# Linear attention on one core: loads with 64 reads of 8 KB and 128 writes of 4 KB

## The chip, the cores and the metric

The kernel runs on one core of a Trainium2 chip. The metric is device time in microseconds (us) of one execution; lower is better. A core has five engines with queues of their own (PE: matrix products and weight loads; DVE: vector work; ACT: activation functions; POOL; SP, which here only issues transfers) and 16 DMA engines that move data between memory (HBM) and the on-chip SBUF of 128 partitions.

## The reference

For each of 32 heads, with q, k, v of 2048 x 128 in bf16:

```python
phi_q = where(q > 0, q + 1, exp(q)) + 1e-6
phi_k = where(k > 0, k + 1, exp(k)) + 1e-6
kv  = einsum("sd,se->de", phi_k, v)          # 128 x 128 per head
z   = phi_k summed over s                    # 128 per head
out = (phi_q @ kv) / (phi_q @ z + 1e-6)
```

## The kernel before

One head is one unit of work. Its k, v and q are loaded with one transfer each of 512 KB: partition p holds rows 16p to 16p+15 of the head, 4 KB in one run (`rows`). k_sb, v_sb and q_sb have six buffers each (`NBI`), o_sb has ten (`NBO`).

For one head: ACT computes exp(k) into ek_sb (L368); DVE makes emk_sb = min(exp(k), 1) + 1e-6 (L382); POOL makes rk_sb = relu(k) (L372) and adds emk_sb to it for some of the 16 row tiles (L390), so that phi_k = emk + rk enters PE either as a sum or as two products. PE accumulates kv and z in kvz_ps (L413, L320; a column of ones beside v gives z); ACT copies them to kvs_sb (L430). PE transposes q into xT_ps (L436); ACT and DVE make emq_sb and rq_sb from it (L447, L454, L456, L468). PE multiplies both with kvs_sb into o_ps (L483, L484), DVE takes the reciprocal of the denominator and divides (L506 to L524; for the last two heads ACT divides part of it, L536), and SP stores o_sb (L571).

The order on each engine comes from keys: `Plan.add` takes an operation with a key, each engine runs its operations in the order of their keys, and waits between engines are derived from the buffers that operations read and write. All loads and stores are issued by SP from one queue, in the order of their keys. A load of head h has a key about six heads ahead and waits until its buffer is free. A store's key grows faster than the heads, so that stores are put off more and more behind loads:

```python
late = h + 1.0 + 0.18 * h
```

The store of head 29 is in three parts of 51, 13 and 64 partitions (`PARTS`), that of head 31 in two halves by columns. After its last issue SP waits for all stores to land (L226).

The loads are made by `load` (L361 is its `dma_start`), called for k, v and q of every head; v's buffer has a gap of 32 columns (`GAP`) of which one column of ones is used.

Of the kernel before, what the change touches and what calls it, by code (L numbers as in the profile page):

```python
# [7 lines left out]
P = 128  # L8
# [4 lines left out]
def _ap(base: bass.AP, elem_offset: int, dims):  # L13
    return bass.AP(base.tensor, base.offset + elem_offset, [list(base.ap[0])] + [list(d) for d in dims])
# [217 lines left out]
def bass_standalone__linear_attn_elu__prompt_kernel(  # L232
# [6 lines left out]
    B, H, S, D = q.shape  # L239
    assert D == P and S == 16 * P  # L240
    NT = 16
# [13 lines left out]
    EVEN, ODD = tuple(range(0, NT, 2)), tuple(range(1, NT, 2))  # L255
    MORE = (4, 6, 8, 10, 12, 14)
    GAP = 32
    VW = NT * D + GAP

    qf = q.rearrange("b h s d -> (b h) s d")  # L260
# [4 lines left out]
    with ExitStack() as es:  # L265
        def sb(name, shape, dt):
            return es.enter_context(nc.sbuf_tensor(name, shape, dt))

        k_sb = sb("k_sb", [P, NBI, NT * D], bf16)
        v_sb = sb("v_sb", [P, NBI, VW], bf16)  # L270
        q_sb = sb("q_sb", [P, NBI, NT * D], bf16)
# [29 lines left out]
        pl = Plan()  # L301

        def rows(x, h):
            return x[h].rearrange("(p j) d -> p (j d)", j=NT)
# [11 lines left out]
               reads=[("id0",)], writes=[("ident",)])  # L316
        pl.add("pool", -7, lambda g: g.memset(_ap(vfull, 0, [[VW, NBI], [1, GAP]]), 1.0), writes=[("vones",)])

# [32 lines left out]
        for h in range(NH):  # L351
# [3 lines left out]
            bi, b2, b3, bo = h % NBI, h % 2, h % 3, h % NBO  # L355

            def load(name, buf, src, key, h=h, bi=bi):
                dst, rws = buf[:, bi], rows(src, h)
                if name == "v":
                    dst = v_sb[:, bi, GAP:]  # L360
                pl.add("sp", key, lambda sp: sp.dma_start(dst, rws), writes=[(name, bi)] + ([("vo", bi)] if name == "v" else []), dma=(name, bi))  # L361

            load("k", k_sb, kf, h - NBI - (1.0 if h < 3 else 1.85 if h == 3 else 1.95))
            load("v", v_sb, vf, h - NBI - 0.8)
            load("q", q_sb, qf, h - NBI - 0.9)

            pl.add("act", at("ek", -2.8),
                   lambda a, bi=bi, b2=b2: a.activation(ek_sb[:, b2, :], k_sb[:, bi, :], ACT.Exp),  # L368
# [36 lines left out]
            def kv(pe, tiles, start=False, stop=False, h=h, bi=bi, b3=b3, both_of=both_of):  # L405
                for j in tiles:
                    both = j in both_of or (j in ODD and j not in ADD and h > 0)
                    for src in (emk_sb, rk_sb) if both else (rk_sb,):
                        first, fin = start and j == tiles[0] and src is (emk_sb if both else rk_sb), stop and j == tiles[-1] and src is rk_sb
                        w = src[:, b3, j * D:(j + 1) * D]  # L410
                        l = j == 0 or (j in ODD and h > 0)
                        c = GAP + j * D
                        last = pe.matmul(kvz_ps[:, 1 - l:NC], lhsT=w, rhs=v_sb[:, bi, c - l:c + D], start=first, stop=fin,  # L413
# [11 lines left out]
            if h:  # L425
                pl.add("pool", h + 0.6, lambda g, bi=bi: g.memset(_ap(vfull, bi * VW + GAP + D - 1, [[2 * D, NT // 2], [1, 1]]), 1.0),
                       reads=[("v", bi)], writes=[("vo", bi)], kind="vo")
# [187 lines left out]
```

## Time and profile before

| | |
|---|---|
| time, median of 3 runs | 168.16 us (167.96 to 168.21) |
| the profiled execution | 167.82 us, of which the span of the profile is 166.5 us |
| moved over the DMA queue of SP | 67.12 MB in 18592 packets: 50.33 MB read from HBM, 16.78 MB written to it |
| mean rate over the span | 404 GB/s |
| busy | PE 94%, DVE 91%, ACT 93%, POOL 64% of the span |
| a load or a store, issue to landing, median | 15 us |

The span runs from the first instruction to the last event of the program. "Busy" leaves out waiting and issuing. A DMA packet in the records is one piece of one transfer on one DMA engine: 128 pieces of 4 KB for a transfer of 512 KB, eight on each of the 16 engines, and one small packet per engine that raises the semaphore. A transfer has landed when all 16 engines have raised it.

### The profile page before, as it was taken

The page shows a single profiled execution, that of the slowest core. Times are in us where ns is not written, and L with a number is a line of the kernel's source. Part 1 is how long each engine was busy: PE and PEld are TensorE (multiplying, and loading weights), DVE is VectorE, ACT ScalarE, POOL GpSimd, SP SyncE. Part 2 cuts the span into 40 slices and gives each one's busy share as a digit, 9 for nine tenths or more (in the row PEclk, how much of TensorE's full clock was granted, in tenths as well). Part 3 has the DMA queues.
Part 4 walks back from the last instruction along what each step waited for, and adds up shares of the span by engine and source line. Part 5 has one row for each costly group of instructions (what it writes and reads, how often), then busy time and mean ns, then how long its engine had stood idle before and what let it go on. Part 6 is the DMA issues. An engine that isn't in the chain of part 4 may idle for free.

```text
span 166.5 us, 6269 instructions
## 1 busy us (share of the span) xinstructions
PE 156.0 (94%) x2819; PEld 145.3 (87%) x2453; DVE 152.3 (91%) x270; ACT 155.0 (93%) x143; POOL 106.3 (64%) x128
## 2 busy tenths in 40 slices
PE   7789999999999999999999999999999999999960
PEld 0259999999999999899999989999998999999950
DVE  0587999999999999999999999999999999999991
ACT  3979999999999999999999999999999999998790
POOL 2405788676767877676778867676787767677300
PEclk9999999999999999999999999999999999999998
DMA  5999999999999999999999999999999999999986
GB/s 205 345 417 421 413 415 419 412 407 418 417 416 419 422 417 417 422 421 411 424 420 414 423 421 415 419 421 415 422 420 416 422 421 418 418 421 418 415 310 239
DMA packets 18605, 67.25 MB, mean 404 GB/s; under 512 B 2082, under 2 KB 2210, under 8 KB 18594
## 3 DMA queue, kind: packets, MB, share of 16 engines
q1 hardware_dynamic: 18592, 67.12, 99.4%
q8 instruction: 5, 0.08, 0.2%
q14 instruction: 6, 0.05, 0.1%
q10 hardware_dynamic: 2, 0.00, 0.0%
HBM read 50.33 MB, written 16.78 MB: 403 GB/s over the span
## 4 chain that ended last, share of the span: by engine, by line
DVE 58%; PE 17%; POOL 12%; ACT 6%; issue 3%; DMA 2%; DVEq 0%
DVE o_sb L524 20%; POOL rk_sb L390 12%; DVE rq_sb L456 11%; DVE emk_sb L382 10%; DVE emq_sb L468 9%; PE kvz_ps L413 6%; PE o_ps L483 5%; PE o_ps L484 5%; ACT ek_sb L368 3%; DVE rden_sb L512 3%; DVE o_sb L517 3%; ACT eq_sb L447 2%; DMA k_sb<-in_k_dram 2%; DVE den_sb L506 2%; DVE rk_sb L390 1%
## 5 line engine op out<-in xcount | busy, mean ns | idle before, releaser
L413 PE MATMUL kvz_ps<-v_sb,rk_sb 128*128 128x129 bf16 (+1 forms) x512 | 67.0, 220 | 2.8 <-DVE rk_sb L390 1.0
L524 DVE TENSOR_TENSOR o_sb<-o_ps,rden_sb 128x768 bf16<-128x768 f32 (+2 forms) x62 | 67.8, 1135 | 0.0
L390 POOL TENSOR_TENSOR rk_sb<-rk_sb,emk_sb 128x640 bf16<-128x640 bf16 x30 | 41.9, 1395 | 39.5 <-DVE emq_sb L468 38.2
L372 POOL TENSOR_SCALAR rk_sb<-k_sb 128x1024 bf16<-128x1024 bf16 (+1 forms) x60 | 64.1, 1068 | 2.5 <-DMA k_sb<-in_k_dram 2.5
L483 PE MATMUL o_ps<-kvs_sb,emq_sb 128*128 128x129 bf16 (+1 forms) x536 | 65.2, 217 | 0.0
L484 PE MATMUL o_ps<-kvs_sb,rq_sb 128*128 128x129 bf16 (+1 forms) x536 | 64.4, 217 | 0.0
L368 ACT ACTIVATE ek_sb<-k_sb 128x2048 bf16<-128x2048 bf16 x32 | 61.0, 1907 | 2.6 <-DMA k_sb<-in_k_dram 2.6
L447 ACT ACTIVATE eq_sb<-xT_ps 128x2048 bf16<-128x2048 bf16 (+1 forms) x33 | 60.0, 1821 | 2.0 <-PE xT_ps L436 2.0
L413 PE MATMUL kvz_ps<-v_sb,emk_sb 128*128 128x129 bf16 (+1 forms) x338 | 53.3, 221 | 0.6 <-DVE emk_sb L382 0.3
L413 PEld LDWEIGHTS kvz_ps<-v_sb,rk_sb 128*128 128x128 bf16 x512 | 46.1, 98 | 7.6 <-POOL rk_sb L390 2.7
L483 PEld LDWEIGHTS o_ps<-kvs_sb,emq_sb 128*128 128x128 bf16 x536 | 51.2, 98 | 0.8 <-issue 0.3
L484 PEld LDWEIGHTS o_ps<-kvs_sb,rq_sb 128*128 128x128 bf16 x536 | 51.3, 98 | 0.0
L436 PE MATMUL xT_ps<-ident,q_sb 128*128 128x128 bf16 x512 | 33.8, 219 | 0.6 <-DMA q_sb<-in_q_dram 0.4
L436 PEld LDWEIGHTS xT_ps<-ident,q_sb 128*128 128x128 bf16 x512 | 29.9, 98 | 5.1 <-DMA q_sb<-in_q_dram 4.2
L413 PEld LDWEIGHTS kvz_ps<-v_sb,emk_sb 128*128 128x128 bf16 x338 | 32.5, 98 | 0.9 <-DVE emk_sb L382 0.5
L320 PE MATMUL kvz_ps<-ones_sb,rk_sb 128*128 128x1 bf16 x232 | 31.3, 165 | 0.0
L454 ACT ACTIVATE rq_sb<-xT_ps 128x1024 bf16<-128x1024 bf16 x30 | 30.9, 1029 | 0.0
L382 DVE TENSOR_SCALAR emk_sb<-ek_sb 128x2048 bf16<-128x2048 bf16 x32 | 22.0, 688 | 5.6 <-ACT ek_sb L368 5.6
L456 DVE TENSOR_SCALAR rq_sb<-xT_ps 128x1024 bf16<-128x1024 bf16 x34 | 23.3, 690 | 1.1 <-PE o_ps L484 1.0
L468 DVE TENSOR_SCALAR emq_sb<-eq_sb 128x2048 bf16<-128x2048 bf16 x32 | 22.1, 690 | 0.0
L320 PE MATMUL kvz_ps<-ones_sb,emk_sb 128*128 128x1 bf16 x121 | 19.9, 166 | 0.0
L430 ACT ACTIVATE kvs_sb<-kvz_ps 128x129 bf16<-128x129 f32 x32 | 9.0, 281 | 1.6 <-PE kvz_ps L413 0.9
(28 smaller groups left out, 49.2 us busy)
## 6 DMA issues: line engine op xcount, KB each, us to landing
k_sb<-in_k_dram SPq DMA_DIRECT2D x32, 512.0 KB, 15.0
q_sb<-in_q_dram SPq DMA_DIRECT2D x32, 512.0 KB, 15.1
v_sb<-in_v_dram SPq DMA_DIRECT2D x32, 512.0 KB, 15.1
out_dram<-o_sb SPq DMA_DIRECT2D x30, 512.0 KB, 15.3
out_dram<-o_sb SPq DMA_DIRECT2D x1, 288.0 KB, 3.7
out_dram<-o_sb SPq DMA_DIRECT2D x1, 256.0 KB
out_dram<-o_sb SPq DMA_DIRECT2D x1, 224.0 KB, 3.6
out_dram<-o_sb SPq DMA_DIRECT2D x1, 204.0 KB
```

Source lines behind the costliest of these rows:

```text
L320: return pe.add_instruction(mybir.InstMatmult(start_tensor_calc=start, stop_tensor_calc=stop, ldweights=False, bass_skip_group_check=True, ...
L368: lambda a, bi=bi, b2=b2: a.activation(ek_sb[:, b2, :], k_sb[:, bi, :], ACT.Exp),
L372: pl.add(eng, key, lambda e: e.tensor_scalar(rk_sb[:, b3, c], k_sb[:, bi, c], BIG, 0.0, op0=ALU.min, op1=ALU.max), reads=[("k", bi)] + ([( ...
L382: lambda d, b2=b2, b3=b3: d.tensor_scalar(emk_sb[:, b3, :], ek_sb[:, b2, :], 1.0, EPS, op0=ALU.min, op1=ALU.add),
L390: return e.tensor_tensor(out=a, in0=a, in1=b, op=ALU.add)
L413: last = pe.matmul(kvz_ps[:, 1 - l:NC], lhsT=w, rhs=v_sb[:, bi, c - l:c + D], start=first, stop=fin, skip_group_check=True)
L436: last = pe.transpose(xT_ps[:, j * P:(j + 1) * P], q_sb[:, bi, j * P:(j + 1) * P], ident[:])
L447: halves[part] = pl.add("act", key, lambda a: a.activation(eq_sb[:, b2, c], xT_ps[:, c], ACT.Exp), reads=both[part:part + 1] or both, writ ...
L456: f = lambda d: d.tensor_scalar(rq_sb[:, b3, c], xT_ps[:, c], 0.0, None, op0=ALU.max)
L483: pe.matmul(o_ap, lhsT=emq_sb[:, b3, t * P:(t + 1) * P], rhs=kvs_sb[:, b3, c0:c1], start=True, stop=False)
L484: return pe.matmul(o_ap, lhsT=rq_sb[:, b3, t * P:(t + 1) * P], rhs=kvs_sb[:, b3, c0:c1], start=False, stop=True)
L524: pl.add("dve", key, lambda d: d.tensor_tensor(out=o_sb[:, bo, 3 * g0:3 * g1, :].rearrange("p (a b) d -> p a b d", b=3), in0=_ap(full, bas ...
```

## The change

The 96 loads are issued as instructions that are written out, with their own access patterns for source and destination. The destination stays 128 partitions of 4 KB. The source, which is contiguous in HBM for one head, is now described as 64 pieces of 8 KB, each of which holds what two neighbouring partitions receive. Stores are as before, and so are keys, buffers, semaphores and waits.

```diff
+    READS = 64
...
             def load(name, buf, src, key, h=h, bi=bi):
-                dst, rws = buf[:, bi], rows(src, h)
-                if name == "v":
-                    dst = v_sb[:, bi, GAP:]
-                pl.add("sp", key, lambda sp: sp.dma_start(dst, rws), writes=[(name, bi)] + ([("vo", bi)] if name == "v" else []), dma=(name, bi))
+                row = v_sb[:, bi, GAP:] if name == "v" else buf[:, bi]
+                step, n = row.ap[0][0], P // READS
+                dst = bass.AP(row.tensor, row.offset, [[step, P], [1, NT * D]])
+                whole = src[h]
+                rws = bass.AP(whole.tensor, whole.offset, [[n * NT * D, READS], [1, n * NT * D]])
+
+                def f(sp):
+                    return sp.add_instruction(mybir.InstDMACopy(
+                        mode="Copy", queue="qSPDynamicHW", name=nc.get_next_instruction_name(), engine=mybir.EngineType.SP,
+                        ins=sp.lower_ap_dma(rws), outs=sp.lower_ap_dma(dst)))
+                pl.add("sp", key, f, writes=[(name, bi)] + ([("vo", bi)] if name == "v" else []), dma=(name, bi))
```

## The prediction

> **What bounds the kernel now.** I read the page first: engines, the 40 slices and the DMA queue.
>
> ```profile
> span 166.5 us, 6269 instructions
> ...
> PE 156.0 (94%) x2819; PEld 145.3 (87%) x2453; DVE 152.3 (91%) x270; ACT 155.0 (93%) x143; POOL 106.3 (64%) x128
> ...
> DMA  5999999999999999999999999999999999999986
> GB/s 205 345 417 421 413 415 419 412 407 418 417 416 419 422 417 417 422 421 411 424 420 414 423 421 415 419 421 415 422 420 416 422 421 418 418 421 418 415 310 239
> ...
> q1 hardware_dynamic: 18592, 67.12, 99.4%
> ```
>
> Four engines and the DMA all look full. The page alone doesn't say which of them sets the end. Look at the GB/s row: flat near 418 from the third slice to the last but two, whatever the engines do. Next, the waits between 15 and 155 us, longest first:
>
> ```profile
> POOL rk_sb L390 <- DVE emq_sb L468: 38.2, 29, 1.5
> PEld kvz_ps L413 <- POOL rk_sb L390: 2.7, 11, 0.3
> PEld kvz_ps L413 <- issue: 1.4, 5, 0.4
> POOL rk_sb L390 <- DVE emk_sb L382: 1.2, 1, 1.2
> ```
>
> No engine waits for a load there. Loads of k and q land 3 to 5 us before their use from head 8 on. So in the middle DVE and ACT set the pace: one head every 4.75 us in the chain. But a head moves 2.10 MB (three loads and a store of 512 KB), and at 418 GB/s that takes 5.02 us. The queue loses 0.27 us per head and makes up for it with its lead at the start and with stores that are put off. Who pays for that is seen in stretches of time (length, PE, PEld, DVE, ACT, POOL busy, PE clock, DMA share, GB/s):
>
> ```profile
> 140.00:150.00 10.00, 9.93 (x189) 9.65 (x165) 9.83 (x19) 9.96 (x9) 7.28 (x9) 1.00 1.03 420
> 155.00:160.00 5.00, 4.77 (x92) 4.46 (x79) 4.86 (x11) 4.63 (x10) 0.93 (x2) 1.00 1.02 396
> 160.00:163.00 3.00, 1.08 (x20) 0.90 (x16) 2.73 (x10) 2.63 (x10) 0.00 (x0) 1.00 0.78 289
> 163.00:167.00 4.00, 0.00 (x0) 0.00 (x0) 0.00 (x0) 0.00 (x0) 0.00 (x0) 0.82 0.49 191
> ```
>
> Compute ends at 162.84; then 3.6 us in which half the DMA engines still work. SP's own waits after 136 us, and its last issues:
>
> ```profile
> SPq L226 <- DMA out_dram<-o_sb: 3.0, 2, 2.4
> ```
> ```profile
> 160.94 2.30 SPq L571 DMA_DIRECT2D out_dram<-o_sb  x3
> ```
>
> The trace keeps each DMA's 16 landings, one per DMA engine. The store of head 28 lands from 159.06 to 163.08: eight engines are through by 159.43, the last is 4 us behind. The last store (issued 162.87) lands on ten engines by 164.94, on the others from 165.42 to 166.48. From the packet records an engine has its pieces back to back (starts 155 ns apart) from about 2 us to its end. So the end, 166.5, is set by lagging DMA engines that work off a queue, not by the last division. If all were as early as the first ten, the span would be 164.9. **That is the room: 1.5 to 1.7 us at the end, open to anything that shortens a load on a DMA engine.** It also makes the kernel sensitive the other way: 96 loads of 8 pieces per engine, so each ns added to a 4 KB piece costs 96 x 8 = 768 ns.
>
> **The change part by part.** Order, waits and every compute instruction stay; only line numbers move. Of each of the 96 loads, the writes stay 128 pieces of 4 KB, the reads go from 128 of 4 KB to 64 of 8 KB: per DMA engine 4 reads and 8 writes in place of 8 and 8.
>
> *Price of a piece.* The trace has three sizes in the same stream, stores of the last heads included. Spacing of starts on one engine: 4096 bytes 155.3 ns, 2304 bytes 89.4, 1792 bytes 70.4. Slope: (155.3 - 70.4) / 2304 = 0.0368 ns per byte; what is left per piece: 155.3 - 150.9 = 4.4 ns (and 89.4 - 84.9 gives 4.5). All these had equally many reads and writes, so the trace doesn't say on which side the 4.4 ns lie. If they come with the read (one packet per read), a load saves 4 x 4.4 = 17.6 ns per engine, and 96 loads save 1.69 us. If the write has them too, the two sides overlap and nothing is saved. The other end: the only 8 KB pieces in the trace, fetches of instructions on queue 14, took 309 ns where two of 4 KB are recorded at 159 each; 9 ns per pair makes 36 ns per load and 3.4 us in all (both sides were 8 KB there, and it is the length of a record, not a spacing). I take 1.69 us, in the middle and from the spacing. The Trainium skill, DMA: Bandwidth & Descriptors, "Why small descriptors are slow (HBM only)", puts about 3 cycles on each packet on the bus between the read and the write half, and says that joining pieces pays only at 256 bytes or less. With that skill page's 850 MHz this is an estimate of 3.5 ns per piece, 1.35 us in all and a time of 166.8; the trace's 4.4 ns is of that kind, and the advice that it isn't worth it would hold only where no queue sets the end.
>
> *Where it shows.* Not in the middle: there loads just land earlier, at most 1.7 us by head 31. At the end the laggards, continuously busy, come 1.69 us earlier: 166.48 becomes 164.79. Two things stop it there. The last store can't land before its issue at 162.87 plus what its first ten engines took, 164.94. And head 29's store in parts (51 partitions, which three engines carry at 17 pieces each) is issued from 157.20 to 157.93, when its data are ready; those three engines, which I take for the landings at 165.42 to 165.97, could start its pieces only about 1.0 us earlier than now, 165.0. So the span goes to about 165.0: a gain of 1.5.
>
> *The start.* The first load is on the chain one to one: issued 0.73, landed 4.07, ACT starts 4.09; q of head 0 at 5.3 and k of head 1 at 8.97 are waited for too. The first pieces took 205 to 444 ns. Bounds: if an 8 KB read must be complete before its write, one more piece of about 155 ns, +0.16 to +0.3 over the first loads; if the read rate alone improves, 1.1% of 8 us, -0.1. I take 0, nearer the second row since reads and writes of a piece overlap in the stream.
>
> *SP.* An unblocked issue is 0.39 to 0.47 us; stores of 51, 13 and 128 partitions take 0.33, 0.32 and 0.33. The number of pieces hardly matters: 0. If issues became 1 us, k of head 0 would pay 0.6 once; the others hide behind 1.25 us of transfer each.
>
> Sum: -1.5 against the profiled execution, 167.82 (span 166.5 and 1.3 around it): 166.3. That execution lies 0.34 below the median, so against 168.16: **166.7**.
>
> **Rivals.** (1) *The write side sets the pace*: 8 writes of 4 KB keep their 155.3 ns, and nothing changes but the start: 168.1, within 0.3. For it: nothing in the trace tells the two sides apart. Against: a stream in which one side had no fixed cost would need only the other side's. Chance 0.15.
>
> (2) *The engines lose their own ports*: slower. In the trace an engine's pieces run at 155 ns beside 15 others, so the 128-to-128 loads are dealt out without collisions. Where the partitions are not all 128, it collides: while the last 64 partitions of head 29's store are read (159 to 160.5 us), pieces take 300 to 441 ns in place of 159. If 64 reads over 128 writes are dealt out in simple order, eight neighbouring partitions per engine, two engines would share a place about half the time: 1.5 x 1.256 = 1.9 us per load, 6.9 us per head, some 225 us in all. It decides from 0.45 ns per piece on (0.34 us). The Trainium skill, SBUF — State Buffer, "Door 1: The DMA port swizzle", gives each port partitions p to p+3 and p+32 to p+35, so a dealing by neighbours would straddle two ports; the 300 ns pieces agree, but no run here shows how uneven counts are dealt. Against it: both counts split evenly into 16. Chance 0.14.
>
> (3) *Long reads start later*: the +0.3 of the start, or slower HBM reads in longer runs, without the gain: 168.6. Chance 0.11.
>
> **How the numbers follow.** Forecast 0.60, its own range 166.2 (the whole 1.7 and 0.2 at the start) to 167.6 (a third of the saving). The range reaches to 168.9 to take in rivals 1 and 3 with the spread of the runs (0.25 us); it leaves out rival 2 and little else. 0.2%, or 0.34 us, is about what a measurement of this kernel can tell from none. Faster 0.60; same 0.15; slower 0.14 + 0.11 = 0.25.
>
> **What would show it.** Right: GB/s in the middle from 418 to 421 to 424; head 28's store lands 1.5 to 2 us earlier on its last engine; the stretch after compute shrinks from 3.6 to about 2.1 us; compute still ends at 162.8. Wrong: the same GB/s and the same tail (rival 1); GB/s well below 418, and DMA waits of ACT or PE in the middle (rival 2); the first load landing after 4.2 (rival 3). The forecast also fails if the tail shrinks by less than loads gained, because the parts of head 29 hold it.

## The result, and the profile after

The changed kernel takes 168.66 us (median of 7 runs, 168.08 to 168.81) beside 168.00 us of the kernel before (167.91 to 168.21, 7 runs, same chip): ratio 1.0032, 95% interval 1.0019 to 1.0046. It is slower by 0.3% where a gain of 0.9% was forecast. The first profiled execution, 168.08 us, was the shortest of the seven; a later one of the same kernel took 168.63 us, close to the median. Both are read here, the second as the usual one.

Did the loads change as said? The page of the first:

```profile
span 166.8 us, 6269 instructions
...
q1 hardware_dynamic: 12448, 67.12, 98.1%
```

The same bytes in 6144 packets fewer, 64 for each of 96 loads. The stretches of time of the usual execution (length, five engines' busy time, PE clock, DMA share, GB/s), with the middle of before for comparison:

```profile
40.00:150.00 110.00, 108.46 (x2032) 105.04 (x1777) 107.74 (x187) 108.72 (x93) 79.47 (x93) 1.00 1.02 422
...
155.00:160.00 5.00, 4.77 (x91) 4.46 (x78) 4.82 (x11) 4.36 (x9) 1.21 (x2) 1.00 0.90 354
160.00:163.00 3.00, 1.35 (x25) 1.17 (x22) 2.90 (x10) 2.91 (x11) 0.00 (x0) 1.00 0.80 254
163.00:167.50 4.50, 0.00 (x0) 0.00 (x0) 0.10 (x1) 0.00 (x1) 0.00 (x0) 0.69 0.46 178
```
```profile
40.00:150.00 110.00, 108.45 (x2032) 105.04 (x1777) 107.77 (x185) 108.67 (x93) 79.67 (x93) 1.00 1.03 419
```

In the middle the engines do exactly what they did, and the transfers run faster: 422 GB/s in place of 419. Between 155 and 160 us it is the other way: 354 where before had 396. The lead is given back there. SP's waits after 150 us, in the usual execution:

```profile
SPq L579 <- DVE o_sb L532: 8.8, 2, 4.4
SPq L226 <- DMA out_dram<-o_sb: 3.5, 3, 2.7
```

And in before:

```profile
SPq L571 <- DVE o_sb L524: 8.8, 2, 4.4
```

8.8 us go into waiting for the results of the last heads, in both: the last load has been issued by then (at 135.79 us in before, 132.18 in the usual execution), and what is left is stores whose data are not there yet. And the wait for the last landings, forecast to shrink, is 3.5 us where before had 3.0.

The start has changed as well. SP's first issues, before and after:

```profile
0.73 0.39 SPq L361 DMA_DIRECT2D k_sb<-in_k_dram  x1
1.18 0.42 SPq L361 DMA_DIRECT2D q_sb<-in_q_dram  x1
1.64 0.43 SPq L361 DMA_DIRECT2D v_sb<-in_v_dram  x1
2.11 0.43 SPq L361 DMA_DIRECT2D k_sb<-in_k_dram  x1
```
```profile
0.73 0.57 SPq L366 DMA_DIRECT2D k_sb<-in_k_dram  x1
1.36 0.57 SPq L366 DMA_DIRECT2D q_sb<-in_q_dram  x1
1.98 0.60 SPq L366 DMA_DIRECT2D v_sb<-in_v_dram  x1
```

An issue takes 0.57 to 0.60 us in place of 0.39 to 0.43. The fourth, k of head 1, goes out at 2.62 in place of 2.11 (third and fourth rows: v of head 0, k of head 1). The chain of the usual execution goes through it:

```profile
2.62 6.66 DMA k_sb<-in_k_dram
9.28 0.02 issue
9.30 1.92 ACT ek_sb L376
```

In before k of head 1 landed at 8.97 and ACT began it at 8.99. ACT is 0.31 late there, and compute ends 0.26 late: 163.10 for 162.84.

Four numbers carry the rest; they are worked out from the trace's packet records and landings. *Stream*: by how much the bytes landed at 40 and at 150 us lag behind those of before, in us at 418 GB/s (negative: ahead; a packet counts when it is whole). *Slowest DMA engine*: when the last of the 16 engines lands the store of head 28; the landings carry no engine number. *Compute end* is DVE's or ACT's last instruction, *last landing* that of the last store.

| kernel (profiled execution) | stream at 40 / 150 | slowest engine, head 28 | compute end | last landing |
|---|---|---|---|---|
| before, 167.82 | 0 / 0 | 163.08 | 162.84 | 166.48 |
| after, 168.08 | +0.11 / -0.93 | 163.14 | 163.79 | 166.74 |
| after, 168.63 | +0.40 / -0.61 | 164.01 | 163.10 | 167.29 |

So the long reads bring the stream forward by 1.04 and 1.01 us between 40 and 150 us. But it starts 0.1 to 0.4 us late, and the slowest DMA engine is no earlier than before or even 0.9 us later. The table doesn't show why; the experiments do.

### The profile page after: what moved, and what is told of

The parts are those of the page before. It is cut to its first block, busy times and chain, and to the rows that moved or that the text cites. A ratio compares the mean times of both kernels' runs of the same rounds, so it can differ in the third digit from the quotient of the medians.

```text
span 166.8 us, 6269 instructions
## 1 busy us (share of the span) xinstructions
PE 156.7 (94%) x2819; PEld 146.2 (88%) x2453; DVE 152.2 (91%) x270; ACT 154.8 (93%) x143; POOL 106.3 (64%) x128
## 4 chain that ended last, share of the span: by engine, by line
DVE 57%; PE 19%; POOL 12%; ACT 4%; DMA 3%; issue 2%; SPq 0%; DVEq 0%
DVE o_sb L532 20%; POOL rk_sb L398 12%; DVE rq_sb L464 11%; DVE emq_sb L476 9%; DVE emk_sb L390 9%; PE kvz_ps L421 6%; PE o_ps L491 5%; PE o_ps L492 5%; DVE rden_sb L520 3%; DMA q_sb<-in_q_dram 3%; DVE o_sb L525 3%; ACT eq_sb L455 2%; ACT ek_sb L376 2%; DVE den_sb L514 2%; PE xT_ps L444 2%
## 5 line engine op out<-in xcount | busy, mean ns | idle before, releaser
L444 PE MATMUL xT_ps<-ident,q_sb 128*128 128x128 bf16 x512 | 34.6, 222 | 1.5 <-DMA q_sb<-in_q_dram 1.5
L444 PEld LDWEIGHTS xT_ps<-ident,q_sb 128*128 128x128 bf16 x512 | 30.7, 99 | 5.8 <-DMA q_sb<-in_q_dram 5.4
```

Source lines behind the costliest of these rows:

```text
L444: last = pe.transpose(xT_ps[:, j * P:(j + 1) * P], q_sb[:, bi, j * P:(j + 1) * P], ident[:])
```

## The experiments

The theories. **Issue**: the written-out instruction is not the one that `dma_start` builds. In the built program the latter carries a mark (`ant_dge_precooked`) and the former doesn't; without it SP needs longer, the first loads come later, and an end that hangs on a lagging DMA engine is later too. **Long reads**: the first 8 KB pieces cost the start, and 64 reads against 128 writes disturb something later. **Tail**: the reads do gain, but the end can't use it.

**Half of the change at a time.** `even_start` loads heads 0 to 2 by `dma_start` and the other 87 loads with 64 reads; `uneven_start` is its reverse; `reads128` writes all loads out, with 128 reads; `writes256` has 128 reads and 256 writes of 2 KB.

```diff
 # even_start; uneven_start has h >= 3, reads128 has READS = 128 and no such line
+                    if h < 3:
+                        return sp.dma_start(row, rows(src, h))
 # writes256
+                dst = bass.AP(row.tensor, row.offset, [[step, P], [NT * D // 2, 2], [1, NT * D // 2]])
```

> The nine loads of heads 0 to 2 are issued in the old form (128 reads, 128 writes), the other 87 read 64 pieces. Theory: the loss sits in the first 16 us (longer issues on SP, a later first piece) and the gain in the last 4 us. Then the first load lands at 4.1 us, compute ends at 162.8 to 163.0, the stretch after it is 2.8 to 3.1 us as in the changed kernel, span 165.7 to 166.0, time 167.2 to 167.5: faster than before by 0.3% to 0.5%. Rival (the changed loads cost something in the middle or hold the slowest DMA engine, whatever the start): compute ends late all the same or the tail is 3.6 us again, time 168.0 to 168.6.

> The mirror image: heads 0 to 2 read 64 pieces, the other 87 loads are in the old form. Theory: the start costs 0.9 to 1.0 us as in the changed kernel, nothing is gained on the DMA engines: compute ends at 163.7 to 163.9, rate in the middle 418 GB/s, time 168.6 to 169.2. Rival: the start costs little by itself and the time is that of before, 168.0.

> The written-out instruction with 128 reads of 4 KB, even counts. Theory: the longer issue comes from the unequal counts, so an unblocked issue is 0.39 to 0.47 us again, the first load lands at 4.1 and the time is 168.0, the same as before. Rival: the written-out instruction itself costs it: issues of 0.57 to 0.60 us, the first load lands at 4.25 to 4.3, time 168.2 to 168.6.

> Unequal counts the other way: 128 reads of 4 KB, 256 writes of 2 KB. Theory (the 4.4 ns belong to the read; unequal counts make the issue long; long first reads delay the first load by themselves): rate in the middle as before, 417 to 419 GB/s, issues of 0.57 us or more, first load at 4.25 to 4.3 (issue alone, without the 0.15 of a long read), time 168.1 to 168.5. Rival (every write carries a fixed cost as well): 4.4 ns on each 4 KB more, 96 x 8 x 4.4 ns = 3.4 us on every DMA engine, rate 410 GB/s or less, time 171 or more.

Measured, against before on the same chip: `even_start` 167.97 us, 0.9998 [0.9984, 1.0012]; `uneven_start` 168.98, 1.0062 [1.0046, 1.0079]; `reads128` 168.72, 1.0047 [1.0030, 1.0064]; `writes256` 171.46, 1.0192 [1.0161, 1.0223]. The loss is already there in `reads128`, which reads and writes as before and is only written out. Its SP timeline:

```profile
0.73 0.57 SPq L368 DMA_DIRECT2D k_sb<-in_k_dram  x1
```

The same 0.57 us, so the issue's length has nothing to do with 64 against 128. And the loss is gone in `even_start`, where only the first nine loads differ from the changed kernel; but the gain forecast for it (167.2 to 167.5) did not come. With 256 writes the middle runs at 414 GB/s where before had 419:

```profile
40.00:150.00 110.00, 108.55 (x2036) 105.15 (x1776) 107.88 (x185) 108.77 (x93) 79.68 (x93) 1.00 1.03 414
```

Its stream falls back by 1.33 us between 40 and 150 us; 68 loads land in that time, with 8 more writes per engine each: 2.4 ns for a write more. So writes are not free either, but they cost less than a read's 3.8 ns (below). Two things limit this reading. The packet records show the reads alone (16256 packets of 4 KB, as in `reads128`), so that the 256 writes are known only from the access pattern. And the time, 3.5 us above before, is more than 2.4 ns for 8 x 96 writes (1.8 us) and the 0.8 us of `reads128`: in this trace the PE clock was halved once more, from 20.3 to 23.7 us, and compute ended at 166.70. What the rest comes from isn't shown.

**The mark alone.** `no_mark` is the kernel before, word for word, but told to build its instructions without the mark. This takes it from the stores too, so that the loss may be larger than in `reads128`.

```diff
+    nc.dge_precook = False
```

> The kernel before in every access pattern, built so that no transfer carries the mark that dma_start puts on its instruction (ant_dge_precooked), loads and stores alike. Theory: the mark alone makes the difference of 0.18 us between an issue of dma_start and a written-out one. Then issues are 0.57 to 0.60 us, the first load lands at 4.3, compute ends 0.9 to 1.7 us later than before, time 168.5 to 169.0. Rival (something else in the written-out instruction): issues of 0.39 to 0.47 us and 167.9.

169.16 us, 1.0075 [1.0055, 1.0095]. Nothing is written out here and nothing is long, and the issues are those of the changed kernel:

```profile
0.73 0.58 SPq L362 DMA_DIRECT2D k_sb<-in_k_dram  x1
1.37 0.58 SPq L362 DMA_DIRECT2D q_sb<-in_q_dram  x1
1.99 0.60 SPq L362 DMA_DIRECT2D v_sb<-in_v_dram  x1
```

That settles that the mark is what the longer issue and the loss come from. Whether the uneven shape may carry the mark isn't known, and it wasn't tried.

**How many marked loads, how long the others.** `even_start_reads128` and `even_start_reads32` are `even_start` with 128 reads and with 32 of 16 KB; `even_six` has heads 0 to 5 by `dma_start`, `two_even` only k and q of head 0, `even_six_reads32` six heads and 32 reads.

```diff
 # even_six; two_even: h == 0 and name != "v"
-                    if h < 3:
+                    if h < 6:
 # the reads32 kernels
-                step, reads = row.ap[0][0], 64
+                step, reads = row.ap[0][0], 32
```

> The loads of heads 0 to 2 by dma_start, the other 87 written out with 128 reads of 4 KB: the longer issue without the long reads. Theory (the longer issue costs only while the first loads are waited for): the time of before, 167.8 to 168.1. Rival (0.6 us per issue also costs later, and hides the gain of the long reads in even_start): 168.2 to 168.6.

> As even_start, but 32 reads of 16 KB. Theory (3.5 ns per read piece): a load saves 6 x 3.5 = 21 ns on a DMA engine where 64 reads save 14; rate in the middle 422 GB/s (421 with 64 reads, 418 before), the first engines of head 28's store another 0.5 us earlier; time as even_start or up to 0.2 us under it, since the slowest engine and the issue of the last store hold the end. Rival (reads over 8 KB stall the stream, or writes alone set the pace): rate 418 to 421 or less.

> The loads of heads 0 to 5 by dma_start, 78 loads with 64 reads. Theory: the first 16 us are wholly those of before, since the loads in the queue behind the first ones are in the old form too; compute ends at 162.8 to 163.0; the stretch after it is 2.9 to 3.0 us; time 167.3 to 167.7, faster than before by 0.15% to 0.35%. Rival (the start of even_start was already that of before, and its lost 0.3 us is scatter between runs, or the gain after compute does not exist without the profiler): 167.8 to 168.1.

> Only k and q of head 0 are issued by dma_start, the other 94 loads read 64 pieces. Theory: of the first loads these two are the ones on the chain whose landing moved (k0 from 4.07 to 4.42, q0 from 5.29 to 6.43; k of head 1 landed at 8.97 in both kernels), so undoing them undoes nearly the whole loss: compute ends at 162.8 to 163.2, time 167.6 to 168.0, the same as even_start. Rival (the loss is shared by all loads of the first heads): compute ends at 163.4 or later, time 168.2 to 168.6.

> As even_six, with 32 reads of 16 KB in the other 78 loads. Theory: a load saves a little more than with 64 reads (18 against 16 ns on the first engines in the second half of even_start_reads32), the end is held by the slowest DMA engine all the same: 167.4 to 167.7, up to 0.3% faster than before. Rival (the low times of even_start_reads32 were scatter): 167.8 to 168.1.

Medians of 12 runs each: `even_start_reads128` 167.94, 1.0011 [0.9983, 1.0040]; `even_start_reads32` 167.59, 0.9983 [0.9959, 1.0008]; `even_six` 167.71, 0.9993 [0.9978, 1.0008]; `two_even` 168.35, 1.0011 [0.9984, 1.0039]; `even_six_reads32` 167.44, 0.9978 [0.9954, 1.0002]. None of them alone is clear of no change. `even_start_reads128` has the unmarked instruction in 87 of 96 loads and stands at 1.0011, where `reads128`, with all 96, has 1.0047: most of what the missing mark costs, it costs at the start. In the traces the picture is sharper; each row is one execution, and its time stands beside the median of its kernel:

| kernel | time (median) | first loads marked | reads | stream at 40 / 150 | slowest engine, head 28 | last landing |
|---|---|---|---|---|---|---|
| even_start_reads128 | 167.73 (167.94) | yes | 128 | -0.17 / -0.17 | 163.06 | 166.40 |
| even_start | 167.51 (167.97) | yes | 64 | -0.13 / -1.18 | 162.81 | 166.14 |
| even_six | 167.75 (167.71) | yes | 64 | -0.05 / -1.08 | 163.01 | 166.32 |
| even_start_reads32 | 168.17 (167.59) | yes | 32 | +0.11 / -1.25 | 162.66 | 166.83 |
| even_six_reads32 | 167.42 (167.44) | yes | 32 | +0.11 / -1.23 | 162.77 | 166.08 |
| two_even | 168.32 (168.35) | k, q of head 0 | 64 | -0.03 / -1.05 | 163.64 | 166.98 |
| reads128 | 168.85 (168.72) | no | 128 | +0.37 / +0.40 | 163.82 | 167.42 |
| no_mark | 169.00 (169.16) | no | 128 | +0.47 / +0.52 | 164.34 | 167.65 |
| uneven_start | 168.62 (168.98) | no | 128 from head 3 | +0.33 / +0.35 | 164.00 | 167.28 |

Read the stream column in two steps. The mark moves its value at 40 us: by 0.5 to 0.6 with 128 reads, by 0.2 to 0.5 with 64 (+0.11 and +0.40 in the changed kernel for -0.05 and -0.13). The +0.11 with 32 reads lies in the counting, since more of a 16 KB packet is under way at any moment; with the finished share of such packets counted it is -0.14 and -0.22. The number of reads moves the difference between 40 and 150: 0.0 to 0.05 with 128, 1.02 to 1.05 with 64, 1.34 to 1.36 with 32. And the slowest engine follows the mark by 0.8 to 1.3 us (128 reads: 163.82 and 164.34 for 163.06), and the reads by only 0.05 to 0.4 in the marked kernels. So the tail theory holds: most of the gain is on the other engines.

**Relieving the slow engine.** If it is one engine that ends the kernel, dealing out the store of head 28 unevenly might help.

```diff
 # before_28: on the kernel before; even_six_28: on even_six
-    PARTS = {LAST - 2: (51, 13, 64)}
+    PARTS = {LAST - 3: (65, 63), LAST - 2: (51, 13, 64)}
```

> The kernel before with head 28's store in parts of 65 and 63 partitions, all loads in the old form: tells whether that edit pays without the long reads. Theory: the first engines have less time to spare (head 28's store landed at 159.1 on them, 158.0 with long reads), so the nine that get more finish later, and the gain is smaller: 167.6 to 168.0. Rival (the edit alone is what helps): as low as even_six_28.

> As even_six, and the store of head 28 is issued in parts of 65 and 63 partitions, which go to the lowest 13 and 9 of the 16 DMA engines by the rule seen with head 29's parts. Theory (the gain of the loads isn't seen at the end because one DMA engine is some 4 us behind the first ones, at 1.38 us per store instead of 1.25, and it is not one of the lowest): that engine saves up to 8 pieces, 1.2 us, the last store lands 0.5 to 0.9 us earlier after compute's end than in even_six, time 167.0 to 167.4. Rival (the slow engine is among the first 9, or the last store's issue holds the end): no change or later by up to 0.8 us, 167.7 to 168.5.

169.25 (1.0080 [1.0049, 1.0112]) and 169.27 (1.0067 [1.0040, 1.0095]): a loss in both. Compute ended as early as ever (162.48 and 163.09), the stretch after it was 4.9 and 4.0 us. The slowest engine was not relieved: head 28's last landing came at 163.73 and 163.35, for 163.08 in before and 163.01 in `even_six`. Which engine got how many pieces the trace doesn't tell, so that why the edit loses over 1 us is not shown.

**The clock at the start.** In the first trace of the changed kernel something else stood out. PE's warm-up matmuls end at 4.95 us; q of head 0 lands at 6.43, and then the 16 transposes of head 0 are slow. Before, and after (count; min/median/max ns):

```profile
L436 PE MATMUL xT_ps<-ident,q_sb x16: 219/219/230, 5.3 to 6.2; 128*128 128x128 bf16 x16
```
```profile
L444 PE MATMUL xT_ps<-ident,q_sb x16: 287/314/314, 6.5 to 8.1; 128*128 128x128 bf16 x16
```

Full clock was granted from 5.1 us in before, from 9.2 here, and compute ended 0.95 later. It looked like the cause of the loss. The Trainium skill, TensorE: Matmul & The Clock Gate, "Part 1: The HAM clock gate (the "warmup" mystery)", has the clock halved until PE has been busy for a window of about 3.4 us that runs freely, so that the moment varies from run to run; the rows agree in that the moment varies, with grants between 3.8 and 10.4 us over the traces of this case. The test: fill the idle time with warm-up matmuls. `after_warm14` and `reads128_warm14` have 14, `even_six_reads32_warm10` and `before_warm10` have 10.

```diff
-        WARM = ((-9, 9), (-1.22, 4), (-0.27, 3))
+        WARM = ((-9, 14), (-1.22, 4), (-0.27, 3))
```

> The changed kernel with 14 warm-up matmuls of 500 columns ahead of head 0 in place of 9, so that PE works until about 6.4 us, when q lands. If PE's idle time of 1.5 us before q delays the clock: full clock is granted by 7 us at the latest, the 16 transposes of head 0 take about 1.1 us in place of 1.89, compute ends at 163.0 to 163.4 in place of 163.79, and the time falls by 0.3 to 0.7 to about 168.0. If the late grant only goes along with something else: compute still ends at 163.8 and the time stays at 168.6. If the longer warm-up itself runs past q at half clock (14 x 0.42 us from 1.0 is 6.9 us): 0.4 us are lost at the start again, and the time stays within 0.2 of 168.6 in spite of an early grant.

> Written-out loads with 128 reads and 128 writes, and 14 warm-up matmuls in place of 9. It had 168.72 with 9, full clock from 10.4 us and compute end at 164.48. If the late grant is the cause: grant by 7 us, compute end 163.1 to 163.5, time 167.9 to 168.3, which then is what the slower issue alone costs. If not: 168.7 and compute end near 164.4.

> Heads 0 to 5 loaded by dma_start, the other 78 loads with 32 reads of 16 KB, and 10 warm-up matmuls in place of 9 (they end at about 5.3, where q lands at 5.15 to 5.3). The kernel with 9 had eight runs at 167.4 and four at 168.2 to 170.5. If the scatter comes from the clock's grant: the high runs go, median 167.2 to 167.4. If not: the same spread about 167.45, or 0.1 more for a warm-up that ends after q.

> The kernel before with 10 warm-up matmuls in place of 9. It had full clock from 5.1 us in the profiled run, so if that is the usual case nothing is gained: 167.9 to 168.0, compute end 162.8. If its runs above 168.2 are late grants: the same median with less spread. If the tenth matmul delays head 0's transposes: 168.0 to 168.1.

`after_warm14` 168.65 us, 1.0029 [1.0010, 1.0049]; `reads128_warm14` 168.98, 1.0053 [1.0025, 1.0081]; `even_six_reads32_warm10` 167.46, 0.9962 [0.9946, 0.9977]; `before_warm10` 168.06, 0.9998 [0.9971, 1.0026]. In the trace of `after_warm14` the edit did just what it should: clock from 6.3, transposes at speed, compute end at 163.02 for 163.79.

```profile
L444 PE MATMUL xT_ps<-ident,q_sb x16: 219/219/220, 6.6 to 7.4; 128*128 128x128 bf16 x16
```

But the median didn't move: 168.65, and 168.66 with nine warm-up matmuls. So the late clock is real and goes with a late compute end in the executions that have it, and it is not why the kernel is slower. The theory that it is, was mine, and it falls. Only a trace of a usual execution could say what is.

**Second traces.** `after_second` and `after_warm14_second` are the same two kernels, unchanged, once more.

> The changed kernel once more, for the trace of a usual run (median 168.66, span 167.4) beside that of its fastest (168.08, span 166.8). If a usual run is a late clock: full clock from 9 us or later, compute end 163.8 to 164.4 and 3 us after it. If it is the transfers: compute end at 163.1 to 163.4 and a last landing 3.8 to 4.3 us later, by engines that lag. If the first loads: q of head 0 later than 6.43, compute shifted by as much.

> The changed kernel with 14 warm-up matmuls once more (runs at 167.8 to 168.2 and at 168.5 to 169.0; the trace at hand is of a run at 167.93). In a run above 168.5, the clock being granted by 6.8 us: if the transfers lag, compute end 163.0 to 163.4 and a stretch of 3.8 to 4.3 us after it in place of 3.48; if the first loads, q of head 0 after 6.9 in place of 5.77 and compute end later by that.

168.63 and 168.43 us. Both have an early clock, and the first's transposes run at speed:

```profile
L444 PE MATMUL xT_ps<-ident,q_sb x16: 219/219/229, 6.0 to 6.9; 128*128 128x128 bf16 x16
```

Both end compute early (163.10, 163.12) and then have 4.19 and 3.97 us until the last landing: the transfers lag. Set side by side:

| kernel | slowest engine, head 28 | last landing | difference | time |
|---|---|---|---|---|
| after_warm14 | 163.17 | 166.50 | 3.33 | 167.93 |
| after_warm14_second | 163.79 | 167.09 | 3.31 | 168.43 |
| after_second | 164.01 | 167.29 | 3.28 | 168.63 |
| reads128_warm14 | 164.46 | 167.76 | 3.29 | 169.10 |
| even_six_reads32_warm10 | 162.75 | 166.09 | 3.33 | 167.42 |

The difference is 3.3 us in every row. With the kernels above there are 18 traces (without those that split head 28), and in 14 of them, from 162.75 to 167.34 for the landing of head 28, it lies between 3.28 and 3.40. That is what such an engine still has to move: its share of head 29, which takes 0.78 to 0.88 us in these 14, then eight pieces each of head 30 and of the two halves of head 31. By the spacings of the prediction the eight pieces take 8 x 155.3, 8 x 89.4 and 8 x 70.4 ns, or 1.24, 0.72 and 0.56 us. The last landing of each of these three comes 1.22 to 1.29, 0.69 to 0.72 and 0.53 to 0.57 us after that of the store ahead, in all 18 traces: no pause. The other four traces differ in head 29 alone, which takes 1.08 to 2.12 us. Three of them have a late compute end (`after`, `reads128`, `before_warm10`), but the end of compute doesn't hold the last landing there either: the first engines land the last store 1.9 to 2.0 us after its issue, the last of the 16 another 1.0 to 1.3 us later. Why head 29 takes longer in these four is open. **The kernel ends when the slowest DMA engine has worked off its queue.**

How far the last of the 16 landings falls behind can be followed in the usual execution: it is 0.25 us behind the eighth from 7.8 to 16.5 us, 1.13 at 17.8, 1.5 to 1.9 up to 80 us, then steadily more: 2.45 at 105, 3.25 at 131, 4.88 at 159. It need not be the same engine all the time: from 32 to 70 us the fifteenth landing is within 0.04 us of it, and in before within 0.4 from 31 to 142 us. At the store of head 28 it is alone, 3.40 us behind the fifteenth (1.39 in before, 1.38 to 3.45 over the 18 traces).

The step near 17 us is in all 18 traces, with 0.3 to 1.7 us, before's included (from 0.87 to 1.56), and coincides with a fetch of instructions on queue 8, 16 KB in 1.1 us. That these are connected is argued, not shown. The slow growth comes at the stores. Over the last seven or eight stores up to head 28 the last landing moves on by 1.36 to 1.38 us a store where the eighth moves by 1.24 to 1.25, in all 18 traces. For the loads, from 80 to 150 us, the slowest landing moves on by 1.231 to 1.237 us a load with long reads and by 1.238 to 1.247 with 128 (`writes256` left out), the eighth by 1.220 to 1.234 and 1.234 to 1.250. In the means long reads save 16 ns a load on the eighth and 7 on the slowest, and nothing on a store. Why a store takes that engine longer, and why it saves less on a load, no trace names.

**The best version** is `even_six_reads32_warm10`: 167.46 us, 0.9962 [0.9946, 0.9977], the only one that is clear of no change against before, on its own chip. The tenth matmul by itself is worth nothing (`before_warm10`), and without it, on another chip, the median was the same (167.44), with four of twelve runs above 168.1 in place of one.

## Why the prediction was wrong, step by step

- *What bounds the end.* Right in kind: the end was set by DMA engines that work off a queue, not by the last division. The 14 traces with 3.3 us show it far better than the single trace did. Wrong in which: I took three engines loaded by the parts of head 29 to hold the end; the last landing follows from the one that was last with head 28's store already (163.08 in before), with no pause between. In before it is not alone, since two more engines land within 0.11 us of it (166.37 and 166.42 for 166.48).
- *Price of a piece.* Mechanism right, size a little high. Predicted 4.4 ns per read, 17.6 ns a load. Over the whole stream, between 40 and 150 us, 68 loads gained 1.04 us: 15.3 ns a load, 3.8 ns per read. With 32 reads 1.34 us, which is 3.3 ns for each of the six reads less. The estimate from the Trainium skill (DMA: Bandwidth & Descriptors, "Why small descriptors are slow (HBM only)") was 3.5 ns; the measured 3.8 lies between it and mine, the 3.3 with 32 reads just under it. Its advice that joining pieces pays only at 256 bytes or less doesn't hold for the stream here, where joining 4 KB pieces gave 419 to 422 GB/s; for the time of the kernel it was nearly right, for another reason.
- *Where it shows*, the term of -1.5 us. Here the sum failed first. I let the laggards gain the whole 1.69, because all engines looked alike in the packet spacing. The slowest gains 0.05 to 0.4 us where the stream gains 1.04 (marked kernels: 163.06 with 128 reads, 162.66 to 163.01 with fewer). What the landings show of it: a long read's load saves that engine 7 ns in the mean where the eighth saves 16, and it falls back by some 0.13 us at each store at the end, with long reads as without. The stream's lead itself ends at 160 us: from 0.61 ahead at 150 to 0.21, since the stores left are then those that wait for DVE.
- *The floor.* I put it at the first ten engines' landing of the last store, 2.1 us after compute's end. In no trace was the last landing less than 2.94 us after it, since the last engine still had earlier stores to work off.
- *SP*, the term of 0. Wrong, and this turned the sign. I argued that the number of pieces doesn't matter, which is true (`reads128`: 0.57 with 128 pieces), and overlooked that the instruction was another one. Row by row the price is 0.15 to 0.18 us per issue, 0.5 us by the fourth; in the slowest engine's landing 0.8 to 1.3 us; in the time 0.8 (`reads128`, 168.72 for 167.91). I also let all issues but the first hide behind the transfers. But the queue has no slack in which to make up for a late start: `reads128` is 0.37 us behind at 40 us and still 0.40 at 150.
- *The start*, the term of 0, and rival 3. The rival's sign and condition came true (k of head 0 at 4.40 to 4.42, above the 4.2 named), its mechanism only in part: with 128 reads and no mark k lands at 4.34, so most of the delay is the missing mark, and the length of the reads adds less than 0.1. Issues alone don't explain the start, though: q of head 0 went out 0.18 us later and landed 0.69 and 1.14 us later (5.98 and 6.43 for 5.29; 6.43 in `reads128`). Why is open.
- *Rival 1*, the write side. It has a price of its own (2.4 ns per write more, as far as `writes256` shows it) but doesn't set the pace, else the stream had not gained. *Rival 2*, collisions: nothing of it, with 64, 32 or 256 pieces on one side.
- *What would show it.* Of my signs, GB/s came as named (422), the landing of head 28 and the shorter tail did not: 163.14 and 164.01 for 163.08, and 2.95 and 4.19 us for a forecast of 2.1. Compute, forecast to end at 162.8 still, ended at 163.79 and 163.10.
- *The range.* 168.66 lies inside 166.2 to 168.9, but in the part that was added for rivals 1 and 3. Neither one's mechanism made the loss (of rival 3 only the sign and the late first load came true), so that this is luck.

The account for the usual execution: the slowest engine lands head 28 0.93 us later than in before, from then on it is 3.28 in place of 3.40, and the time is 0.81 longer (168.63 for 167.82). In the means of the traces the loss of the mark costs that engine 1.0 us with 128 reads (164.15 for 163.17), and the long reads give back 0.6 of it (163.53 in the four traces of the changed kernel, with nine and with 14 warm-up matmuls).

What stays open: why about 0.5 us of delay in the stream at 40 us becomes 1 us on the slowest engine, and why four traces of nearly the same kernel (`after`, `after_warm14` and their second ones) differ by 0.87 us in its landing. Each trace is one execution.

## What to carry to other kernels

When an instruction is rebuilt by hand to change its shape, first run it by hand with the old shape: what the builder added without a word can cost more than the new shape gains. In a kernel that ends on a lagging DMA engine, as this one does, a faster stream pays only as far as the slowest engine gets faster too, so look at the last of the 16 landings, not at the mean rate or the first landing. And before a conspicuous row of a trace becomes the cause, look whether the traced execution is one of the usual ones.

## What the runs showed of the hardware that was not expected

- A load's issue without the mark holds SP for 0.57 to 0.60 us (64 reads and 128 alike), with it for 0.39 to 0.47. In `no_mark`, where the stores lack it too, the last store's first landing comes 2.77 us after its issue; in the other 17 traces 1.93 to 2.15.
- The last of the 16 DMA engines ends 3.0 to 5.3 us behind the eighth in the store of head 28 (4.88 us in the usual execution, 3.65 in before) in a stream that deals the same bytes to all. Over the last stores up to that one it loses 0.12 to 0.14 us at each.
- Reads and writes of unequal count (64 or 32 against 128, 128 against 256) kept 422 and 414 GB/s in the middle, so that no collisions show; a read costs about 3.8 ns, a write more about 2.4 ns.
- With the same nine warm-up matmuls and an idle time of 1.3 to 1.5 us behind them, PE got its full clock at 9.2 us in one execution of the changed kernel, and at 4.3, before that idle time, in another.
